# Attention and two mixer layers on one core: seven block products in place of eight in the last pair's channel products

## The chip, the cores and the metric

One NeuronCore of a Trainium2 chip runs the whole program in one launch. The metric is the device time in microseconds (us). The engines are named as in the profile: PE (matmul), PEld (PE's weight loads), DVE, ACT, POOL, and SP, which here only issues DMAs.

## The reference

Shapes: batch 4, 12 heads of 64, sequence 448, model width 768, all float32.

```python
scores = cap * tanh((q @ k.T / sqrt(64)) / cap)           # per batch and head
x = softmax(scores) @ v                                   # (4, 448, 768) after joining the heads
theta = x @ w_theta                                       # first mixer layer
y = w_tok_r @ (x * cos(theta)) + w_tok_i @ (x * sin(theta))   # over the tokens
u = x + y
x = u + relu(u @ w_ch)                                    # "wc" in the kernel
h = relu(x.T @ w_tok1) @ w_tok2                           # second layer, over the tokens
u = x + h.T
out = u + relu(u @ w_ch1) @ w_ch2                         # "c1" and "c2"; 768 -> 1536 -> 768
```

## The kernel before

Activations are held with channels on the 128 partitions and the 448 tokens along the row: `XT` holds, for two batches, six chunks of 128 channels. `XHL` holds the same values as two parts, a rounded high part and the rest. Weights are split likewise, and every product of 128x128 weights with a 128x448 chunk is three matmuls (high by high, high by low, low by high; `mm3`). An output chunk of a 768-wide product is six such steps, 18 matmuls in one PSUM bank (`gemm`).

The program goes through attention for all four batches, the mixer layers for batches 0 and 1 (the first pair, woven into the attention of batches 2 and 3), and then the same for batches 2 and 3 (the last pair), which runs alone. `token` is theta and the token mixing of the first layer; `rest` is wc, the second layer's token steps (`tok1`, `tok2`) and three channel groups (`NG`). A group is the c1 product for four output chunks and two batches (8 `gemm`s, 144 matmuls, order `CORD`) and then c2 (6 chunks, two batches, 12 matmuls each). In wc, `wch` makes one output chunk of one batch; `SEQR` is the order in which wc, `tok1` (T), `tok2` (n) and the splits (s) follow each other.

In the first pair each weight is read as raw 8-byte words, converted on ACT, DVE and POOL in pieces of 384 columns, split into high and low and stored to DRAM (`convert`); the last pair reads the split weights back, 768 KB for a unit of 128 output columns, by SP (`unit`, `weight`).

The order of instructions on every engine is made by a list scheduler in the kernel itself (`Plan`): it takes operations as they become ready, by priority, follows limited buffers (`SB` gives the count of each kind: `t` are the exponentials of the attention, 128x896, three to a pair of heads; `w` the weight units; `cw` the conversion pieces; `zx` transposed tokens), and repeats this for 30 rounds, moving work that came late forward. It covers the whole program at once, so a new buffer count or new operations anywhere may change the order elsewhere. `t` buffers are allocated in order; `av` then reads each (value product), POOL or DVE adds it into the first tile of the pair, and `sm` sums the rows.

Of the kernel before, what the change touches and what calls it, by code (L numbers as in the profile page):

```python
# [21 lines left out]
DM = H * D  # L22
P = 128
# [27 lines left out]
CORD = ((0, 0), (1, 0), (0, 1), (2, 0), (1, 1), (3, 0), (2, 1), (3, 1))  # L51
CLOSE = 1
DIR = 12
FRESH = 1
RAWS = 2
CVP = 0
ACCM = 2
# [359 lines left out]
def attn_mix_kernel(ctx: ExitStack, tc: tile.TileContext, kqd, vd, cap, wu, wtok, wt1, wt2, out):  # L417
# [244 lines left out]
    stream = order[:6] + order + order  # L662
    units = {}

    def unit(i):
        for j in range(i, min(i + (FRESH if 6 + DIR <= i < 42 else AHEAD) + 1, len(stream))):
            if j not in units:
                if 6 + DIR <= j < 42:
                    weight("u", stream[j], None, DM // CW)
                    units[j] = open_[stream[j]]  # L670
                    continue
                t = sbuf("w", "w", [2, DM], F32R)
                with pri(-100):
                    weight("u", stream[j], t, DM // CW)
                units[j] = t
        return units[i]

    XT = const("XT", [2, NC6, S])
# [165 lines left out]
        hi(h, src)  # L844
        (lo_pool if XSP[phase[0]] == "p" else lo)(l, src, h)

    def mm3(ps, wfn, xfn, n):
        for k in range(n):
            wh, wl = wfn(k)
            xh, xl = xfn(k)  # L850
            with plan.fuse():
                mm(ps, wh, xh, k == 0, False)
                mm(ps, wh, xl, False, False)
                mm(ps, wl, xh, False, k == n - 1)

    def gemm(ui, i, ps):
        w = unit(ui)
        mm3(ps, lambda k: (w[:, 0, k * P:(k + 1) * P], w[:, 1, k * P:(k + 1) * P]),
            lambda k: (XHL[:, i, k, 0, :], XHL[:, i, k, 1, :]), NC6)

    def token(pr, which):
# [59 lines left out]
            dve.tensor_tensor(out=x, in0=ps, in1=x, op=ALU.add)  # L921

        def usplit(m):
            ws = slice(which[0], which[-1] + 1)
            split(XHL[:, ws, m], XT[:, ws, m, :])

        for op in SEQ[pr].split():
            k, m = op[0], op[1:]
            if k == "w":
                if not WT or pr:  # L930
                    run(tokmix_gen(pr))
            elif k == "u":
                for j in m:
                    usplit(int(j))
            elif k == "t":
                yield from theta(int(m))
            elif k == "z":
                for i in which:
                    zt(int(m), i)
                    yield 0.75  # L940
            else:
                for i in which:
                    mix(int(m), i)
                    yield 4.3

# [8 lines left out]
    def rest(pr):  # L954
        u0 = 12 + pr * len(order)
        load_tok(pr)

        def wch(m, i):
            ps = psum("wc")[:, :S]
            gemm(u0 + m, i, ps)  # L960
            x = XT[:, i, m, :]
            dve.scalar_tensor_tensor(out=x, in0=ps, scalar=0.0, in1=x, op0=ALU.max, op1=ALU.add)
            yield 3.4

        h1s = {}

        def tok1(t, i):
            W1 = WS[1]
            xn = [sbuf("xn", "zx", [1024], F32R)[:CP] for h in range(2)]
            xn = [x.rearrange("p (c j d) -> p c j d", c=NK, j=2) for x in xn]  # L970
            for j in range(2):
                tp = psum("xp")[:CP]
                with plan.fuse():
                    for c in range(NK):
                        pe.transpose(tp[:, c * P:(c + 1) * P], XT[:, i, 2 * t + j, c * CP:(c + 1) * CP], ident)
# [9 lines left out]
            h1 = sbuf("h1", "zx", [2, 512], F32R)  # L985
            act.activation(h1[:, 0, :], ps, AF.Relu)
            dve.scalar_tensor_tensor(out=h1[:, 1, :], in0=ps, scalar=0.0, in1=f(h1[:, 0, :]), op0=ALU.max, op1=ALU.subtract)
            h1s[t, i] = h1
            yield 2.6

        def tok2(t, i):
            h1, W2 = h1s[t, i], WS[2]
            for j in range(2):
                ps = psum("t2")[:, :S]

                def hf(k):
                    s = slice(k * DT + j * P, k * DT + (j + 1) * P)
# [3 lines left out]
                x = XT[:, i, 2 * t + j, :]  # L1001
                dve.tensor_tensor(out=x, in0=ps, in1=x, op=ALU.add)
                yield 1.2

        def usplit(t, i):
            split(XHL[:, i, 2 * t:2 * t + 2], XT[:, i, 2 * t:2 * t + 2, :])

        for op in SEQR.split():
            k, m, i = op[0], int(op[1]), int(op[2])
            if k == "s":  # L1010
                usplit(m, i)
            else:
                yield from {"w": wch, "T": tok1, "n": tok2}[k](m, i)

        for g in range(NG):
            gs = {}
            v0 = u0 + 6 + 2 * FB * g
            for k, i in CORD:
                if k not in gs:
                    gs[k] = sbuf("g", "wg", [2, 2 * S], F32R).rearrange("p a (b s) -> p a b s", s=S)  # L1020
                gt = gs[k]
                ps = psum("c1")[:, :S]
                gemm(v0 + k, i, ps)
                act.activation(gt[:, 0, i], ps, AF.Relu)
                dve.scalar_tensor_tensor(out=gt[:, 1, i], in0=ps, scalar=0.0, in1=f(gt[:, 0, i]), op0=ALU.max, op1=ALU.subtract)
                yield 3.4
            for d in range(NC6):
                def wf(k):
                    n = d * FB + k
                    w = unit(v0 + FB + n // 6)  # L1030
                    s = slice((n % 6) * P, (n % 6 + 1) * P)
                    return w[:, 0, s], w[:, 1, s]

                for i in range(2):
                    ps = psum("c2")[:, :S]
                    mm3(ps, wf, lambda k: (gs[k][:, 0, i, :], gs[k][:, 1, i, :]), FB)
                    x = XT[:, i, d, :]
                    dve.tensor_tensor(out=x, in0=ps, in1=x, op=ALU.add)
                    if g == NG - 1:
                        sp_.dma_start(out[2 * pr + i, d * P:(d + 1) * P, :], x)  # L1040
                    yield 2.3

    def chain(*gens):
        for g in gens:
# [83 lines left out]
```

## Time and profile before

Three runs: median 968.26 us, 967.14 to 968.39.

| What | Value |
|---|---|
| Profiled execution, its own time | 964.5 us |
| Its span, first to last instruction | 962.7 us |
| PE busy | 949.1 us (99%), 4938 matmuls |
| PEld | 731.2 us (76%) |
| DVE, ACT, POOL busy | 532.3 (55%), 444.4 (46%), 188.4 us (20%) |
| DMA | 151.53 MB, mean 157 GB/s |
| PE idle in waits, all its rows summed | 9.7 us |
| PE's last matmul starts | 958.7 us into the span |

How to read it: the page's first part gives shares over the whole span, and the stages differ, so the windows view is read beside it, one line for each stage. PE's matmuls overlap in the records (one lasts some 366 ns, yet 144 of them take about 30 us), so the pace is taken from the length of a run of matmuls and their count.

### The profile page before, as it was taken

The page shows a single profiled execution, that of the slowest core. Times are in us where ns is not written, and L with a number is a line of the kernel's source. Part 1 is how long each engine was busy: PE and PEld are TensorE (multiplying, and loading weights), DVE is VectorE, ACT ScalarE, POOL GpSimd, SP SyncE. Part 2 cuts the span into 40 slices and gives each one's busy share as a digit, 9 for nine tenths or more (in the row PEclk, how much of TensorE's full clock was granted, in tenths as well). Part 3 has the DMA queues.
Part 4 walks back from the last instruction along what each step waited for, and adds up shares of the span by engine and source line. Part 5 has one row for each costly group of instructions (what it writes and reads, how often), then busy time and mean ns, then how long its engine had stood idle before and what let it go on. Part 6 is the DMA issues. An engine that isn't in the chain of part 4 may idle for free.

```text
span 962.7 us, 13126 instructions
## 1 busy us (share of the span) xinstructions
PE 949.1 (99%) x4938; PEld 731.2 (76%) x4938; DVE 532.3 (55%) x920; ACT 444.4 (46%) x702; POOL 188.4 (20%) x166
## 2 busy tenths in 40 slices
PE   9999999998999999999999999999999999999998
PEld 2223566554766776789999999899999889999997
DVE  7997788776776457747666592332623541212122
ACT  7787888788875446525444450332401221010010
POOL 3545233221221111002322250332200000000000
PEclk9999999999999999999999999999999999999999
DMA  7686846565537643247757589411321103323233
GB/s 252 206 273 203 258 141 193 166 209 168 189 107 214 239 117 117 73 120 247 238 184 238 185 269 322 155 66 34 110 72 60 66 1 131 103 95 131 97 121 128
DMA packets 71128, 151.53 MB, mean 157 GB/s; under 512 B 9368, under 2 KB 50456, under 8 KB 71064
## 3 DMA queue, kind: packets, MB, share of 16 engines
q1 hardware_dynamic: 71064, 150.69, 48.9%
q8 instruction: 39, 0.64, 0.3%
q14 instruction: 25, 0.20, 0.1%
HBM read 108.86 MB, written 41.68 MB: 156 GB/s over the span
## 4 chain that ended last, share of the span: by engine, by line
PE 91%; DVE 5%; DMA 2%; ACT 2%; issue 1%; POOL 0%; SPq 0%; DVEq 0%; ACTq 0%
PE c L401 36%; PE tm L401 10%; PE wc L401 9%; PE th L401 9%; PE av L401 7%; PE t L401 6%; PE sp L401 6%; PE sm L401 2%; PE tp L401 2%; DMA dn<-sr 2%; PE xp L401 2%; DVE cw L401 1%; ACT t L401 1%; DVE raw L401 1%; DVE w L401 1%
## 5 line engine op out<-in xcount | busy, mean ns | idle before, releaser
L401 PE MATMUL c<-g,w 128*128 128x448 f32 x864 | 177.2, 366 | 0.0
L401 PE MATMUL c<-XHL,w 128*128 128x448 f32 x846 | 175.6, 368 | 0.0
L401 PEld LDWEIGHTS c<-g,w 128*128 128x128 f32 x864 | 162.3, 188 | 13.9
L401 PEld LDWEIGHTS c<-XHL,w 128*128 128x128 f32 x846 | 158.7, 188 | 16.1 <-issue 0.7
L401 POOL TENSOR_TENSOR cw<-cw,raw 128x384 uint32<-128x384 uint32 (+2 forms) x94 | 92.3, 982 | 330.5 <-DVE cw L401 166.3
L401 PE MATMUL tm<-WT,zn 128*128 128x448 f32 x483 | 107.6, 372 | 2.3 <-ACT zn L401 1.8
L401 ACT ACTIVATE g<-c 128x448 fp32r<-128x448 f32 x47 | 25.7, 546 | 173.9 <-PE c L401 173.9
L401 PEld LDWEIGHTS tm<-WT,zn 128*128 128x128 f32 x483 | 88.3, 188 | 17.6 <-issue 3.5
L401 PE MATMUL th<-XHL,w 128*128 128x448 f32 x432 | 96.4, 372 | 0.0
L401 DVE TENSOR_TENSOR XT<-c,XT 128x448 f32<-128x448 f32 x72 | 44.8, 623 | 87.4 <-PE c L401 87.4
L401 PEld LDWEIGHTS th<-XHL,w 128*128 128x128 f32 x432 | 79.5, 188 | 14.9 <-issue 5.7
L401 PE MATMUL wc<-XHL,w 128*128 128x448 f32 x414 | 88.1, 368 | 0.0
L401 PEld LDWEIGHTS wc<-XHL,w 128*128 128x128 f32 x414 | 76.9, 188 | 9.6 <-issue 2.5
L401 DVE SCALAR_TENSOR_TENSOR g<-c,g 128x448 fp32r<-128x448 f32 x47 | 29.3, 622 | 99.3 <-ACT g L401 99.2
L401 ACT ACTIVATE t<-sp,consts 128x896 f32<-128x896 f32 x72 | 72.2, 1004 | 21.9 <-PE sp L401 20.5
L401 ACT ACTIVATE t<-t,consts 128x896 f32<-128x896 f32 x72 | 75.1, 1042 | 1.7
L401 PE MATMUL av<-t,vt 128*64 128x448 f32 x288 | 66.3, 558 | 0.0
L401 DVE SCALAR_TENSOR_TENSOR cw<-raw,cw 128x384 uint32<-128x384 uint32 (+2 forms) x94 | 64.3, 685 | 2.7
L401 PE MATMUL sp<-kq 64*128 64x448 f32 (+1 forms) x240 | 59.2, 574 | 2.6 <-DVE xr L401 1.9
L401 ACT CAST w<-cw 128x384 fp32r<-128x384 f32 x72 | 35.1, 508 | 45.2 <-POOL cw L401 16.5
L401 DVE TENSOR_TENSOR w<-cw,w 128x384 fp32r<-128x384 f32 x72 | 48.8, 693 | 7.2 <-ACT w L401 7.1
L401 PEld LDWEIGHTS av<-t,vt 128*64 128x64 f32 x288 | 15.8, 135 | 38.9 <-issue 35.7
(132 smaller groups left out, 1138.7 us busy)
## 6 DMA issues: line engine op xcount, KB each, us to landing
w<-cu SPq DMA_DIRECT2D x54, 768.0 KB
raw<-wu SPq DMA_DIRECT2D x72, 384.0 KB
cu<-w SPq DMA_DIRECT2D x72, 384.0 KB
kq<-kqd SPq DMA_DIRECT2D x24, 448.0 KB
vt<-vd SPq DMA_DIRECT2D x24, 224.0 KB
out<-XT SPq DMA_DIRECT2D x24, 224.0 KB
dn<-sr SPq DMA_DIRECT2D x18, 224.0 KB
raw<-wtok SPq DMA_DIRECT2D x14, 224.0 KB
```

Source lines behind the costliest of these rows:

```text
L401: getattr(eng[o.eng], name)(*map(real, a), **{x: real(y) for x, y in k.items()})
```

## The change

In the last pair, wc and c1 take their output chunks two at a time, (j, j+3) in wc and (k, k+2) in c1, for both batches together: a 2x2 block of outputs whose sum over the six input chunks is cut into two halves of three. A is the weight block (input half, output chunk), B the activation block (input half, batch). Instead of 8 block products of 9 matmuls there are 7 (`fast`), in Winograd's form of Strassen's algorithm:

- S1 = A21+A22, S3 = A11-A21, S2 = S1-A11, S4 = A12-S2 from the weights (`combine`: four reads of stored unsplit weights, 128x384 each, four POOL adds, then a high part on ACT and a low part on POOL or DVE for each), anew for every block.
- T3 = B22-B12, T2 = T3+B11, T4 = B21-T2, T1 = B12-B11 from `XT` (`sums`, `first`), split into high and low; made once for wc and once for c1, and kept in buffers that the attention has left, T1 over a part of `XHL` that the block before has finished with.
- The products, in order: A11 B11, A12 B21, S2 T2, S1 T1, S3 T3, S4 B22, A22 T4. Each is 9 matmuls in its own PSUM bank. One ACT copy and seven DVE adds combine them; then the four results go on as before.

The first block of wc and the first block of group 0 of c1 stay as four plain `gemm`s (72 matmuls), batch 1 first. So two blocks of wc and five of c1 are made by `fast`. c2 is unchanged (`mixed_group`; `FASTC2` is 0 and what it switches isn't run).

With it go: `convert` also stores the unsplit piece of 14 of the units 6 to 23; the token steps take chunks (t, t+3) together in the last pair (`both`), splits there are made for each chunk and batch alone; z and mixing take batch 1 first (`ZO`); `SEQR` has its own order for the last pair, in which W10 runs all of block 1 and W21 one product of block 2; `h1` moves from the `zx` buffers to `wg`. Buffer counts: `t` 4 to 3, `w` 3 to 4, `cw` 2 to 3, `zx` 4 to 5; `FRESH`, how many converted units are asked for ahead, 1 to 2.

```diff
-SB = {'kq': 2, 'vt': 2, 'hl': 1, 't': 4, 'tm': 2, 'sv': 2, 'dn': 1, 'xr': 2, 'pk': 3, 'rq': 2, 'w': 3, 'raw': 3, 'cw': 2, 'wg': 4, 'zx': 4, 'rc': 4}
+SB = {'kq': 2, 'vt': 2, 'hl': 1, 't': 3, 'tm': 2, 'sv': 2, 'dn': 1, 'xr': 2, 'pk': 3, 'rq': 2, 'w': 4, 'raw': 3, 'cw': 3, 'wg': 4, 'zx': 5, 'rc': 4}
-SEQR = "w00 w01 w10 w11 w20 w21 T00 w30 w31 T01 n00 w40 w41 T10 n01 w50 w51 s00 s01 T11 n10 T20 n11 s10 s11 T21 n20 n21 s20 s21"
+SEQR = ('w00 w01 w10 w11 w20 w21 T00 w30 w31 T01 n00 w40 w41 T10 n01 w50 w51 s00 s01 T11 n10 T20 n11 s10 s11 T21 n20 n21 s20 s21', 'W00 W10 T00 W21 T01 W21 n00 W21 n01 W21 T10 W22 T11 W20 s01 s00 n10 T20 n11 s11 s10 T21 n20 n21 s21 s20' if FASTWC else 'w00 w01 w10 w11 w20 w21 T00 w30 w31 T01 n00 w40 w41 T10 n01 w50 w51 s00 s01 T11 n10 T20 n11 s10 s11 T21 n20 n21 s20 s21')
+SWC = ("+ raw raw raw".split(), "+ 2 2".split())
...
+SC1 = ("+ raw raw raw".split(), "+ rc rc zx".split()) if FASTC2 else ("zx rc zx rc".split(), "zx rc zx rc".split())
+ZO = (1, 0)
+TE = "vvvp"
+TL = "vvvv"
...
+FE = "pppp"
+SL = "ppvv"
...
-FRESH = 1
+FRESH = 2
...
 def convert(key, raw, rows, n):
...
     wv = f(wv)
+        if key[0] == "u" and key[1] in plain:
+            if key[1] not in whole:
+                whole[key[1]] = dram(f"f{key[1]}", P, [DM])
+            sp_.dma_start(whole[key[1]][:, key[2] * n:(key[2] + 1) * n], wv)
...
+    def quad(a, c, fast):
+        return [("u" if not fast else "c", a, full(a)), ("u" if not fast else "c", c, half(c) if fast else full(c))]
+        stream += quad(6, 9, 0) + quad(7, 10, 1) + quad(8, 11, 1)
+    for g in range(NG):
+        n = 12 + g * FB
+        stream += quad(n, n + 2, g > 0) + quad(n + 1, n + 3, 1)
+            stream += [("u", i, full(i)) for i in order[12 + 2 * FB * g + FB:12 + 2 * FB * (g + 1)]]
+    plain = set(range(6 if FASTWC else 12, 36 if FASTC2 else 24)) - {6, 9, 12, 14}
...
+    def sums():
...
+        for k in range(H3):
+            b11, b12, b21, b22 = (XT[:, i, o + k, :] for o, i in ((0, 0), (0, 1), (H3, 0), (H3, 1)))
...
+            for e, o, x, y, op in ((TE[0], t[3], b22, b12, ALU.subtract), (TE[1], t[2], t[3], b11, ALU.add), (TE[2], t[4], b21, t[2], ALU.subtract)):
+                (pool if e == "p" else dve).tensor_tensor(out=o, in0=x, in1=y, op=op)
+            for j in (2, 3, 4):
+                h, l = pairs[f"t{j}"][k]
+                hi(h, t[j])
+                (lo_pool if TL[j - 1] == "p" else lo)(l, t[j], h)
...
+    def combine(t, srcs, N):
+        x = {}
+        with pri(-100):
+            for j, src in zip((2, 0, 1, 3), srcs):
+                x[j] = sbuf("F", "cw", [CW])[:, :N]
+                sp_.dma_start(x[j], src)
...
+        add(FE[0], s1, s3, s1)
+        add(FE[1], s3, s2, s3, ALU.subtract)
+        add(FE[2], s2, s1, s2, ALU.subtract)
+        add(FE[3], s4, s4, s2, ALU.subtract)
+        for j in (1, 2, 0, 3):
+            h, l = t[j]
+            hi(h, x[j])
+            (lo_pool if SL[j] == "p" else lo)(l, x[j], h)
...
+    def fast(A, T, post):
+        def prod(ps, a, b, first=True, last=True):
+            mm3(ps, lambda k: tuple(x[:, k * P:(k + 1) * P] for x in A[a]), lambda k: T[b][k], H3, first, last)
...
+        act.copy(p1, one("11", "b11"))
+        post(0, 0, plus(p1, one("12", "b21")))
+        dve.tensor_tensor(out=u2, in0=one("s2", "t2"), in1=p1, op=ALU.add)
+        p5 = one("s1", "t1")
+        u4 = plus(u2, p5)
+        ps = one("s3", "t3")
+        dve.tensor_tensor(out=u2, in0=ps, in1=u2, op=ALU.add)
+        post(1, 1, plus(u2, p5))
+        post(0, 1, plus(u4, one("s4", "b22")))
+        post(1, 0, plus(u2, one("22", "t4")))
...
+        def wchs(j):
...
+                for n in range(4):
+                    ps = psum("wc")[:, :S]
+                    if n == 0:
+                        T[0] = sums()
+                    gemm(u0 + n % 2, 1 - n // 2, ps)
...
+                    if n == 1:
+                        first(T[0])
+                        A4[1] = weights4(u0 + 2, SWC[0])
...
+            for n, c in enumerate(fast(A4[j], T[0], post)):
+                if n == 2 and j + 1 < H3:
+                    A4[j + 1] = weights4(u0 + 2 * j + 2, SWC[j])
...
+        def both(t):
+            return (t, t + H3) if pr and FASTWC else (2 * t, 2 * t + 1)
```

## Rows read from the trace of the kernel before

**Rows 1.** busy time of each engine by stage (windows view), columns named first

```profile
core 0: us, PE busy (x) PEld busy (x) DVE busy (x) ACT busy (x) POOL busy (x), PEclk, DMA share, GB/s
0.00:94.00 94.00, 91.14 (x455) 24.99 (x455) 81.78 (x161) 73.60 (x94) 44.13 (x39) 1.00 0.73 236
94.00:411.00 317.00, 312.18 (x1707) 208.93 (x1708) 222.99 (x390) 229.34 (x338) 66.47 (x57) 1.00 0.54 168
411.00:591.00 180.00, 180.00 (x882) 162.76 (x881) 113.74 (x196) 75.77 (x156) 49.97 (x46) 1.00 0.70 218
591.00:698.00 107.00, 106.42 (x556) 96.68 (x555) 41.93 (x65) 35.95 (x66) 27.86 (x24) 1.00 0.34 117
698.00:782.00 84.00, 82.29 (x481) 75.63 (x480) 32.60 (x48) 15.68 (x24) 0.00 (x0) 1.00 0.17 57
782.00:963.00 181.00, 177.11 (x866) 162.21 (x864) 39.21 (x63) 14.05 (x25) 0.00 (x0) 1.00 0.32 107
```

**Rows 2.** PE's waits: tile, releaser, us in total, times, longest

```profile
PE sp L401 <- DVE xr L401: 1.9, 1, 1.9
PE tm L401 <- ACT zn L401: 1.8, 2, 1.2
PE t L401 <- DVE h L401: 1.5, 2, 1.0
...
PE sp L401 <- ACT tm L401: 1.0, 1, 1.0
...
PE tm L401 <- DVE zn L401: 0.5, 1, 0.5
```

**Rows 3.** timeline of PE, end of the first pair: start, us, what, count

```profile
532.22 29.91 PE L401 MATMUL c<-XHL,w 128*128 128x448 f32 x144
561.97 29.53 PE L401 MATMUL c<-g,w 128*128 128x448 f32 x144
```

**Rows 4.** instruction groups by shape: busy us, mean ns, idle before

```profile
L401 POOL TENSOR_TENSOR cw<-cw,raw 128x384 uint32<-128x384 uint32 x72 | 75.6, 1050 | 263.2 <-DVE cw L401 138.4 <-issue 45.9 <-ACT raw L401 27.4
...
L401 DVE TENSOR_TENSOR w<-cw,w 128x384 fp32r<-128x384 f32 x72 | 48.8, 693 | 7.2 <-ACT w L401 7.1
L401 DVE TENSOR_TENSOR XT<-c,XT 128x448 f32<-128x448 f32 x72 | 44.8, 623 | 87.4 <-PE c L401 87.4
...
L401 ACT CAST w<-cw 128x384 fp32r<-128x384 f32 x72 | 35.1, 508 | 45.2 <-POOL cw L401 16.5 <-issue 12.5 <-PE c L401 8.1
...
L401 DVE TENSOR_TENSOR XHL<-XT,XHL 128x896 fp32r<-128x896 f32 x18 | 20.5, 1142 | 10.0 <-ACT XHL L401 10.0
...
L401 POOL TENSOR_TENSOR XHL<-XT,XHL 128x448 fp32r<-128x448 f32 x12 | 14.8, 1234 | 18.5 <-DVE XHL L401 18.5
...
L401 DVE TENSOR_TENSOR XHL<-XT,XHL 128x448 fp32r<-128x448 f32 x12 | 9.2, 784 | 1.6 <-ACT XHL L401 1.6
```

**Rows 5.** timeline of DVE, end of the last pair's token mixing

```profile
680.82 3.06 DVE L401 TENSOR_TENSOR XHL<-XT,XHL 128x896 fp32r<-128x896 f32 x2
683.80 0.62 DVE L401 TENSOR_TENSOR XT<-tm,XT 128x448 f32<-128x448 f32 x1
...
690.14 1.09 DVE L401 TENSOR_TENSOR XHL<-XT,XHL 128x896 fp32r<-128x896 f32 x1 [0.29 <-ACT XHL L401]
```

**Rows 6.** timeline of POOL, the same stretch

```profile
681.69 5.42 POOL L401 TENSOR_TENSOR rc<-rc,XT 128x448 f32<-128x448 f32 x4 [13.71 <-issue]
```

**Rows 7.** timeline of all engines, attention of one pair of heads

```profile
52.92 2.16 POOL L401 TENSOR_TENSOR t<-t,t 128x896 f32<-128x896 f32 x1
...
55.75 0.99 ACT L401 ACTIVATE t<-sp,consts 128x896 f32<-128x896 f32 x1
...
56.81 1.28 PE L401 MATMUL sm<-t,ones 128*32 128x448 f32 x6
...
59.16 1.00 ACT L401 ACTIVATE t<-sp,consts 128x896 f32<-128x896 f32 x1
...
63.77 0.97 PE L401 MATMUL av<-t,vt 128*64 128x448 f32 x4
```

**Rows 8.** DMA issues: destination, source, count, size

```profile
w<-cu SPq DMA_DIRECT2D x54, 768.0 KB
```

More of the change, by code (lines that the diff above doesn't have):

```diff
@@ L666, in unit @@
         for j in range(i, min(i + (FRESH if 6 + DIR <= i < 42 else AHEAD) + 1, len(stream))):
[L667 to L675, printed above, removed]
+            if j not in units and (j == i or stream[j][0] == "u"):
+                stream[j][2](j)
         return units[i]
@@ L845, in split, with mm3 @@
         (lo_pool if XSP[phase[0]] == "p" else lo)(l, src, h)
-    def mm3(ps, wfn, xfn, n):
+    def mm3(ps, wfn, xfn, n, first=True, last=True):
         for k in range(n):
@@ L851, in mm3, with first @@
             with plan.fuse():
-                mm(ps, wh, xh, k == 0, False)
+                mm(ps, wh, xh, first and k == 0, False)
                 mm(ps, wh, xl, False, False)
-                mm(ps, wl, xh, False, k == n - 1)
+                mm(ps, wl, xh, False, last and k == n - 1)
+    H3 = NC6 // 2
+    def first(pairs):
+        for k in range(H3):
+            t1 = sbuf("tf", TT[0], [S])
+            (pool if TE[3] == "p" else dve).tensor_tensor(out=t1, in0=XT[:, 1, k, :], in1=XT[:, 0, k, :], op=ALU.subtract)
+            h, l = pairs["t1"][k]
+            hi(h, t1)
+            (lo_pool if TL[0] == "p" else lo)(l, t1, h)
@@ new lines, in combine @@
+    def combine(t, srcs, N):
+        x = {}
+        with pri(-100):
+            for j, src in zip((2, 0, 1, 3), srcs):
+                x[j] = sbuf("F", "cw", [CW])[:, :N]
+                sp_.dma_start(x[j], src)
+        s1, s2, s3, s4 = (x[j] for j in range(4))
+        add = lambda e, o, x, y, op=ALU.add: (pool if e == "p" else dve).tensor_tensor(out=o, in0=x, in1=y, op=op)
+        add(FE[0], s1, s3, s1)
[6 more added lines that the diff above has]
+            (lo_pool if SL[j] == "p" else lo)(l, x[j], h)
@@ new lines, in fast2, with into @@
+    def fast2(A, T, e, close):
+        X = lambda h, i: XT[:, i, e + H3 * h, :]
+        def prod(ps, a, b, first=True, last=True):
+            mm3(ps, lambda k: tuple(x[:, k * P:(k + 1) * P] for x in A[a]), lambda k: T[b][k], 2, first, last)
+        def into(x, y, e="v"):
+            (pool if e == "p" else dve).tensor_tensor(out=x, in0=y, in1=x, op=ALU.add)
+        pa = psum("P")[:, :S]
+        prod(pa, "11", "b11", True, True)
+        p1 = sbuf("p1", "sv", [S])
+        act.copy(p1, pa)
+        for n, x in enumerate((X(1, 1), X(1, 0), X(0, 1))):
+            into(x, p1, XP[n])
+        yield 1.2
+        pd = psum("P")[:, :S]
+        prod(pd, "s4", "b22")
+        into(X(0, 1), pd)
+        yield 1.2
+        pb = psum("P")[:, :S]
+        prod(pb, "s2", "t2", True, True)
+        into(X(0, 1), pb)
+        yield 1.2
+        pc = psum("P")[:, :S]
+        prod(pc, "s1", "t1")
+        into(X(0, 1), pc)
+        close(0, 1, X(0, 1))
+        into(X(1, 1), pc)
+        yield 1.2
+        prod(pb, "s3", "t3", False, True)
+        into(X(1, 1), pb)
+        close(1, 1, X(1, 1))
+        yield 1.2
+        prod(pa, "12", "b21", False, True)
+        into(X(0, 0), pa)
+        close(0, 0, X(0, 0))
+        yield 1.2
+        prod(pb, "22", "t4", False, True)
+        into(X(1, 0), pb)
+        close(1, 0, X(1, 0))
+        yield 1.2
@@ L856, in gemm @@
+    un = [0]
     def gemm(ui, i, ps):
         w = unit(ui)
-        mm3(ps, lambda k: (w[:, 0, k * P:(k + 1) * P], w[:, 1, k * P:(k + 1) * P]),
+        mm3(ps, lambda k: (w[0][:, k * P:(k + 1) * P], w[1][:, k * P:(k + 1) * P]),
             lambda k: (XHL[:, i, k, 0, :], XHL[:, i, k, 1, :]), NC6)
@@ L923, in usplit @@
         def usplit(m):
+            if pr:
+                for i in ZO:
+                    split(XHL[:, i, m], XT[:, i, m, :])
+                return
             ws = slice(which[0], which[-1] + 1)
@@ L937, in token @@
             elif k == "z":
-                for i in which:
+                for i in (ZO if pr else which):
                     zt(int(m), i)
@@ L941, in token @@
             else:
-                for i in which:
+                for i in (ZO if pr else which):
                     mix(int(m), i)
@@ L974, in tok1 @@
                     for c in range(NK):
-                        pe.transpose(tp[:, c * P:(c + 1) * P], XT[:, i, 2 * t + j, c * CP:(c + 1) * CP], ident)
+                        pe.transpose(tp[:, c * P:(c + 1) * P], XT[:, i, both(t)[j], c * CP:(c + 1) * CP], ident)
                 tv = tp.rearrange("p (c d) -> p c d", d=P)
@@ L1000, in tok2 @@
                 mm3(ps, hf, lambda k: (W2[0][:, k, :], W2[1][:, k, :]), 2)
-                x = XT[:, i, 2 * t + j, :]
+                x = XT[:, i, both(t)[j], :]
                 dve.tensor_tensor(out=x, in0=ps, in1=x, op=ALU.add)
@@ L1005, in usplit @@
         def usplit(t, i):
+            if pr:
+                for d in both(t):
+                    split(XHL[:, i, d], XT[:, i, d, :])
+                return
             split(XHL[:, i, 2 * t:2 * t + 2], XT[:, i, 2 * t:2 * t + 2, :])
-        for op in SEQR.split():
+        gens = {}
+        for op in SEQR[pr].split():
             k, m, i = op[0], int(op[1]), int(op[2])
@@ L1011, in rest, with close, plain_group @@
                 usplit(m, i)
+            elif k == "W":
+                if m not in gens:
+                    gens[m] = wchs(m)
+                for _ in range(i or 99):
+                    c = next(gens[m], None)
+                    if c is None:
+                        break
+                    yield c
             else:
                 yield from {"w": wch, "T": tok1, "n": tok2}[k](m, i)
-        for g in range(NG):
+        def close(h, i, x, g, d):
+            if g == NG - 1:
+                sp_.dma_start(out[2 * pr + i, d * P:(d + 1) * P, :], x)
+        def plain_group(g):
             gs = {}
@@ L1043, in chain @@
+        for g in range(NG):
+            yield from (plain_group if not pr else fast_group if FASTC2 else mixed_group)(g)
     def chain(*gens):
```

245 lines of the change are left out of this document (240 added, 5 removed).

## The prediction

> **What bounds the kernel now.** I read the windows view first, cut where one stage gives way to the next: attention alone to 94 us, attention woven with the first pair to 411, that pair's channel groups to 591, then the last pair alone: token mixing to 698, wc and the token steps to 782, channel groups to the end [rows 1]. PE is busy for 91 of 94, 312 of 317, 180 of 180, 106 of 107, 82 of 84 and 177 of 181 us, always at a granted clock of 1.00, the upper of its two levels. So PE sets the time everywhere; work taken off PE is worth its own length while what feeds PE keeps up. The waits view of PE alone comes second: past the first 50 us it has five items of note, 1.9, 1.8, 1.5, 1.0 and 0.5 us [rows 2]. So there is little idle time to win, 6.7 us. In the last pair from 698 us on, where new work is put, DVE is busy for 33 of 84 and 39 of 181 us, ACT for 16 and 14, POOL for none, and the DMA share is 0.17 and 0.32 [rows 1].
>
> **The change, part by part.**
>
> *Matmuls removed.* A block of two output chunks and two batches takes 4 x 18 = 72 matmuls as it stands and 7 x 9 = 63 by the seven products. Two blocks of wc and five of c1 change: 7 x 9 = 63 matmuls fewer. Their pace, from the same kind of product: 144 matmuls from 532.22 to 561.97 us, 29.75 us, 206.6 ns each [rows 3]. 63 x 0.2066 = **13.0 us** off PE. A PSUM group shrinks from 18 matmuls to 9. That costs PE nothing that the rows show: the groups of 12 in c2 run 144 in 29.53 us including the overlap at their end, no slower than the groups of 18 [rows 3].
>
> *Work beside each new block.* A block lasts 63 x 0.2066 = 13.0 us on PE. DVE: seven adds and four results' own operations at 0.623, two low parts of 384 columns at 0.693: 11 x 0.623 + 2 x 0.693 = 8.2 us. POOL: four adds and two low parts of 384 columns at 1.05: 6.3 us. ACT: four high parts at 0.508, a copy and, in c1, four relus: under 5 us [rows 4]. All are below 13.0, so I cost them at nothing; PE covers them. If that cover went, the block would last as long as its DVE work.
>
> *DVE beside POOL.* POOL has been idle here until now, and the two disturb each other: the token mixing's two 896-column low parts took 3.06 us together while POOL multiplied, one alone took 1.09 later, so each lost about 0.44 us [rows 5, 6]. In the same stretch an add with one input from PSUM took its usual 0.62 [rows 5]. In a block six of the 13 DVE operations have both inputs in SBUF: 6 x 0.44 = 2.6 us, 10.8 us in all, still under 13.0. The Trainium skill, SBUF — State Buffer, section Who interferes with whom, states it harder: a DVE instruction with two SBUF inputs contends with a GpSimd instruction that reads SBUF, and the loser fully blocks. By that rule the full 6.3 us of POOL could come on top of DVE's 8.2; the pair of low parts above bears its direction out, not its full price. The case is a rival below.
>
> *T, made twice.* Before the first new block of wc, and again of c1, DVE makes nine sums at 0.62 and twelve low parts at 0.784, and in the same time four results (2.5) and two low parts for the weights (1.4): 5.6 + 9.4 + 2.5 + 1.4 = 18.9 us [rows 4]. What hides it is the plain block, 72 x 0.2066 = 14.9 us, and the two products that use no T, 3.7 us: 18.6 us; T1 has one more, 1.9 us. That is level, but two thirds of T use chunks that are final earlier, when DVE has room (42 of 107 us busy, 33 of 84) [rows 1]. From below it costs nothing; from above, if nothing is made early and POOL's three subtractions at 1.23 and six weight operations at 1.05 (10 us) each block DVE, some 10 us a time [rows 4]. I take 0.5 us a time, near the lower end since DVE is under half busy before both places: **+1.0 us**. Part of it stands for the token steps, whose last results now come by two DVE operations instead of one and whose splits are twelve at 0.784 in place of six at 1.142 (+2.6 us of DVE) [rows 4], beside a PE that waited there for 1.5 us already [rows 2].
>
> *Weights.* A new block reads 768 + 384 KB of split weights and 4 x 192 KB unsplit, 1.97 MB in 13.0 us, 151 GB/s, where two units of 768 KB [rows 8] served 14.9 us (106 GB/s). The last stage moves 107 GB/s now, the first pair's groups 218 beside 180 of 180 us of PE [rows 1]: cost nothing. The unsplit reads, four POOL adds and the parts take about 2 x 1.05 + 0.5 + 1.05 us after landing, and are asked for some five products (9 us) before their use. If a block ran at 107 GB/s it would last 18.4 us.
>
> *Stores in the first pair.* 28 transfers of 192 KB, 5.5 MB over the conversion of 14 units, on SP's queue and behind POOL's result; loads behind them wait with them. The third `cw` buffer covers the longer hold. There PE is never idle, at a DMA share of 0.70 [rows 1]. Cost nothing; from above the 2 us of the largest PE wait there is [rows 2].
>
> *`t` from four buffers to three.* This touches the attention, off the change's own place. In the pair of heads at 55 us a tanh starts at 55.75 into the fourth buffer. With three it would wait until the row sums of the pair before end, 56.81 + 1.28 = 58.09, so 2.3 us late; the tanh at 59.16 is then about 1 us late behind it. The value product of the first reads it at 63.77; tanh and the exp behind it take about 1.0 us each, so it would be done near 60.2, 3.6 us early [rows 7]. So the delay is absorbed and does not pass on. Nine and a half pairs run as densely as this (the first 38 steps, `FIRST`, have nothing woven in). From above, a loss of the 2.3 us in nine pairs would be 20.7 us; from below nothing. I take **+0.5 us**.
>
> *The rest.* `w`, `cw`, `zx` and `FRESH` deeper, other orders, `h1` elsewhere: same instructions. The scheduler orders the whole program anew, so the waits of rows 2 are drawn anew: between -6.7 us (all gone) and about as much more; I take 0, the middle.
>
> **Sum.** 964.5 (the profiled execution's own time) - 13.0 + 1.0 + 0.5 = 953.0. The median of the runs is 968.26, 3.76 above that execution, and the new runs should stand to theirs alike: **956.8 us**.
>
> **Rivals.**
>
> *The new draw wins too.* The deeper buffers end most of the waits of rows 2: up to 6.7 us more, 948 to 953 us. For it: they are waits on DVE and ACT results just ahead of PE, which more buffers let start sooner. Against: two of the five concern the attention, which loses a buffer.
>
> *The seams eat part.* T, splits and token steps crowd DVE around 698 and 782 us, 3 to 5 us at each place: 961 to 966. For it: 18.9 us of DVE work against 18.6 of cover. At the full 10 us a time it is 964.5 - 13.0 + 20 + 0.5 + 3.76 = 976, and slower; it decides above 13 us in all.
>
> *Slower by the attention.* Place: the dense pairs of heads before 94 us. A tanh that waits for the row sums takes its place in ACT's order, ACT is busy for 74 of 94 us and DVE for 82 [rows 1], and if nothing can be put between, PE waits 2.3 us a pair: 953.0 - 0.5 + 20.7 + 3.76 = 977. It decides when PE loses over 13 us, 1.4 us a pair. Against: the 3.6 us that remain at 63.77.
>
> *Weights late.* The saved matmuls turn into waits of PE for S parts: 5.4 us for each of c1's five blocks, 27 us: 983. Against: 218 GB/s in rows 1.
>
> *DVE held by POOL: no gain.* Each of POOL's six operations in a block holds DVE for its whole length: 8.2 + 6.3 = 14.5 us, DVE becomes the bound, and the seven blocks give back 7 x 1.5 = 10.5 of the 13.0 us: 967.3, level with before. The rule of the Trainium skill cited above would have it so. Against: 0.44 us lost per operation in rows 5, and seven of the 13 operations read PSUM.
>
> **How the numbers follow.** Forecast, 953 to 961: 0.60. New draw, 948 to 953: 0.13. Seams in part, 961 to 966: 0.10. DVE held by POOL, level: 0.04. Attention: 0.07. Seams in full: 0.03. Weights: 0.03. A measurement tells a change from none at about 0.2%, 1.9 us. Faster: 0.60 + 0.13 + 0.10 = 0.83; within: 0.04; slower: 0.13. The range 950.5 to 966 holds the forecast, the seams in part and half of the new draw, 0.77, and the ends left out are the slower cases and the best draws.
>
> **What would show it.** PE's matmuls fall from 4938 to 4875 and its busy time by 13 us, nearly all after 698 us. The groups of the first pair run as before. In a new block, runs of 9 matmuls follow without waits, and DVE is busy for 8 to 11 of 13 us, POOL for 6. PE's waits stay near 10 us in sum; new ones name `T` or `S`, low parts, or `zn`, `h` near 698 and 782 us if the seams eat it, `t` or `sp` before 94 us if the attention does, DMA into `cw` if the weights do. The prediction is wrong if the runs come within 2 us of 968, or if the 63 matmuls are gone and PE's idle time has grown by over 5 us.

## The result, and the profile after

The changed kernel's median is **956.69 us** (955.93 to 957.76, four runs) against 968.33 (967.14 to 968.46) for the kernel before on the same chip: a ratio of 0.9883, 95% interval 0.9866 to 0.9900. A second set on another chip gave 955.77 against 964.49, 0.9907 (0.9890 to 0.9924). So it is faster by 0.9 to 1.2%, and the median lies 0.1 us from the forecast. That closeness is partly luck: two of the sum's terms were wrong by almost the same amount in opposite directions, as the stages show.

The profiled execution took 957.76 us, its span is 956.0 us. First the windows view of the kernel after, cut where its own stages give way; the columns are those of [rows 1], its answer in the kernel before.

```profile
core 0: us, PE busy (x) PEld busy (x) DVE busy (x) ACT busy (x) POOL busy (x), PEclk, DMA share, GB/s
0.00:94.00 94.00, 89.48 (x446) 24.54 (x446) 81.76 (x155) 71.30 (x90) 43.05 (x38) 1.00 0.74 239
94.00:411.00 317.00, 311.74 (x1677) 203.87 (x1678) 220.35 (x397) 227.88 (x344) 71.90 (x62) 0.99 0.59 182
411.00:596.80 185.80, 185.80 (x923) 169.29 (x922) 117.19 (x196) 73.67 (x153) 52.34 (x48) 1.00 0.72 226
596.80:706.90 110.10, 107.54 (x557) 98.17 (x556) 53.47 (x83) 42.56 (x82) 33.30 (x29) 0.98 0.34 115
706.90:785.30 78.40, 78.40 (x466) 73.42 (x465) 55.18 (x89) 23.96 (x45) 12.84 (x11) 1.00 0.22 71
785.30:956.00 170.70, 166.78 (x813) 152.29 (x811) 79.76 (x120) 29.33 (x56) 31.44 (x27) 0.99 0.35 115
```

The last pair's theta begins at 596.8 us where it began at 591.3; its mixing lasts 110.1 us where it lasted 106.8; wc and the token steps last 78.4 us (84.2 before), the groups 166.8 us to PE's end (176.8). So from wc on the change gains 15.8 us, more than the 13.0 forecast, and ahead of it 8.8 us are lost. (0.6 us of both figures is only a matter of where the stages are cut: three matmuls of wc now run inside the mixing.) The granted clock is 0.99 in the woven stage (94 to 411 us) and 0.98 in the mixing, where [rows 1] shows 1.00; the 0.99 of the last stage comes from its end, behind PE's last matmul. DVE carries 79.76 us in the last stage (39.21 before), and PE has no idle time there until its last matmul.

The PE timeline of the second block of c1's middle group (start, length, what, how many matmuls) shows the seven products; the first row is A11 B11 and A12 B21 together, the last two lines are A22 T4 and the start of c2.

```profile
854.14 3.88 PE L419 MATMUL P<-XHL,w 128*128 128x448 f32 x18
857.86 2.02 PE L419 MATMUL P<-T,S 128*128 128x448 f32 x9
859.72 2.02 PE L419 MATMUL P<-XHL,S 128*128 128x448 f32 x9
861.58 2.02 PE L419 MATMUL P<-T,S 128*128 128x448 f32 x9
863.44 2.02 PE L419 MATMUL P<-XHL,S 128*128 128x448 f32 x9
865.30 2.02 PE L419 MATMUL P<-T,w 128*128 128x448 f32 x9
867.16 1.99 PE L419 MATMUL P<-g,w 128*128 128x448 f32 x9
```

A product follows every 1.86 us with no wait noted, and the block takes 867.16 - 854.14 = 13.02 us, as priced. The windows view of this block and the one before it:

```profile
841.13:854.14 13.01, 13.01 (x65) 11.83 (x64) 6.50 (x11) 4.18 (x8) 2.03 (x2) 1.00 0.41 122
854.14:867.16 13.02, 13.02 (x65) 11.83 (x64) 9.19 (x14) 3.68 (x7) 5.38 (x5) 1.00 0.46 151
```

DVE is busy for 6.5 and 9.2 of 13.0 us, POOL for 2.0 and 5.4, and the DMA moves 122 and 151 GB/s: everything beside the block fits under it.

The 8.8 us went into PE's waits and into a lower clock behind them. Ahead of theta PE is idle for 9.8 us where it was 7.7, by the windows; 1.7 of the 2.1 us more lie before 94 us (89.48 us busy against 91.14 in [rows 1]). Most of the rest of the 5.5 us is matmuls at the lower clock. PE's largest wait ends at 231.66 us. The timeline of all engines in the kernel after, with what released each idle stretch in brackets:

```profile
230.44 0.62 DVE L419 TENSOR_TENSOR xr<-xr,dn 128x448 f32<-128x448 f32 x1 [4.89 <-DMA dn<-sr]
230.99 0.62 DVE L419 COPY xr<-av 128x448 f32<-128x448 f32 x1
...
231.66 1.76 PE L419 MATMUL sp<-kq 64*64 64x448 f32 x4 [3.49 <-DVE xr L419]
...
233.35 4.52 PE L419 MATMUL th<-XHL,w 128*128 128x448 f32 x12
```

SP had issued that DMA, the softmax denominators of one pair of heads spread over the partitions, at 221.72 us:

```profile
221.72 0.52 SPq L419 DMA_DIRECT2D dn<-sr  x1
```

What it brought was used 8.7 us later. DVE works through its operations in the order that the scheduler gave it: it stood idle for 4.89 us before the one that needs this transfer; behind that one stood the copy that frees a PSUM bank (230.99 us), and PE waited 3.49 us for it. The kernel before waits in the same manner at 224 us, for 1.9 us [rows 2]. DVE's waits for this transfer (waits view: us in total, times, longest), before and after:

```profile
DVE xr L401 <- DMA dn<-sr: 34.8, 11, 4.3
```

```profile
DVE xr L419 <- DMA dn<-sr: 23.3, 10, 5.4
```

So DVE's wait is not new, and it was longer in sum before; new is that PE stood still behind one of them for 3.49 us instead of 1.94. The windows around it:

```profile
225.00:230.00 5.00, 3.17 (x20) 1.91 (x18) 0.56 (x2) 2.67 (x5) 0.00 (x0) 1.00 0.73 210
230.00:236.00 6.00, 4.34 (x11) 2.68 (x12) 5.43 (x11) 2.19 (x4) 0.00 (x0) 0.54 0.40 90
236.00:240.00 4.00, 4.00 (x19) 3.06 (x19) 0.78 (x2) 1.25 (x2) 1.01 (x1) 0.83 0.96 347
```

From about 230.5 us, still inside PE's idle stretch, to about 237.3 us the granted clock was at its lower level (0.5): 12 theta matmuls took 4.52 us where 12 x 0.2066 = 2.5 is the pace of [rows 3], so the wait cost some 2 us more there alone. In the mixing, PE's timeline shows three waits close together, and POOL's (behind it) what they waited for:

```profile
613.25 0.53 PE L419 MATMUL th<-ident,rc 128*128 128x128 f32 x3 [1.14 <-POOL rc L419]
614.33 1.09 PE L419 MATMUL tp<-ident,rc 128*128 128x128 f32 x8 [0.55 <-POOL rc L419]
616.29 9.11 PE L419 MATMUL tm<-WT,zn 128*128 128x448 f32 x36 [0.86 <-ACT zn L419]
```

```profile
609.83 8.96 POOL L419 TENSOR_TENSOR rc<-rc,XT 128x448 f32<-128x448 f32 x8 [17.81 <-ACT rc L419]
```

Here too the clock was at 0.5, from about 616.3 to 619.6 us: 36 matmuls in 9.11 us, against 7.4 at 206.6 ns.

### The profile page after: what moved, and what is told of

The parts are those of the page before. It is cut to its first block, busy times and chain, and to the rows that moved or that the text cites. A ratio compares the mean times of both kernels' runs of the same rounds, so it can differ in the third digit from the quotient of the medians.

```text
span 956.0 us, 13368 instructions
## 1 busy us (share of the span) xinstructions
PE 939.7 (98%) x4875; PEld 721.6 (75%) x4875; DVE 607.7 (64%) x1037; ACT 468.7 (49%) x769; POOL 244.9 (26%) x214
## 4 chain that ended last, share of the span: by engine, by line
PE 76%; DMA 3%; DVE 1%; ACT 0%; issue 0%; SPq 0%; DVEq 0%
PE c L419 29%; PE P L419 10%; PE tm L419 7%; PE th L419 7%; PE wc L419 7%; PE t L419 7%; PE av L419 4%; PE sp L419 3%; DMA dn<-sr 3%; PE xp L419 1%; PE tp L419 1%; DMA sr<-pk 0%; ACT rc L419 0%; DVE xr L419 0%; DVE rc L419 0%
## 5 line engine op out<-in xcount | busy, mean ns | idle before, releaser
L419 PE MATMUL c<-g,w 128*128 128x448 f32 x816 | 168.0, 366 | 0.0
L419 PEld LDWEIGHTS c<-g,w 128*128 128x128 f32 x816 | 153.3, 188 | 13.2
L419 PE MATMUL c<-XHL,w 128*128 128x448 f32 x522 | 108.1, 367 | 0.0
L419 PEld LDWEIGHTS c<-XHL,w 128*128 128x128 f32 x522 | 97.9, 188 | 9.3 <-issue 0.7
L419 DVE TENSOR_TENSOR XT<-c,XT 128x448 f32<-128x448 f32 x68 | 42.4, 623 | 82.7 <-PE c L419 82.6
L419 PEld LDWEIGHTS th<-XHL,w 128*128 128x128 f32 x432 | 81.0, 192 | 15.8 <-issue 5.1
L419 PE MATMUL wc<-XHL,w 128*128 128x448 f32 x306 | 66.4, 370 | 0.0
L419 PEld LDWEIGHTS wc<-XHL,w 128*128 128x128 f32 x306 | 56.5, 188 | 10.8 <-issue 5.3
L419 DVE SCALAR_TENSOR_TENSOR cw<-raw,cw 128x384 uint32<-128x384 uint32 (+2 forms) x94 | 61.7, 657 | 2.6
L419 DVE TENSOR_SCALAR cw<-cw 128x384 uint32<-128x384 uint32 (+2 forms) x94 | 42.0, 447 | 7.4 <-ACT cw L419 7.1
L419 PEld LDWEIGHTS sp<-kq 64*128 64x128 f32 (+1 forms) x240 | 15.9, 164 | 38.4 <-ACT t L419 13.7
```

The source lines that it names most:

```text
L419: getattr(eng[o.eng], name)(*map(real, a), **{x: real(y) for x, y in k.items()})
```

## The experiments

All runs are compared with the kernel before on their own chip (its medians: 968.33 us beside the first run of the changed kernel, 964.70, 963.36 and 964.49 us in the three later sets). Because the whole-program scheduler draws the order anew for each, the stage lengths say more than the totals. They are read off PE's timeline of one profiled execution of each kernel, in us: to the first theta matmul of the last pair, to the end of its mixing, to the end of its token steps, to PE's last matmul.

| Run | Median us | Ratio (95%) | to theta | mixing | wc, tokens | groups |
|---|---|---|---|---|---|---|
| before | | 1 | 591.3 | 106.8 | 84.2 | 176.8 |
| after | 956.69 | 0.9883 (0.9866-0.9900) | 596.8 | 110.1 | 78.4 | 166.8 |
| after_again | 955.77 | 0.9907 (0.9890-0.9924) | 594.7 | 110.2 | 78.4 | 166.8 |
| eighth_product | 967.76 | 1.0037 (1.0024-1.0050) | 595.6 | 111.6 | 82.2 | 176.3 |
| buffers_only | 970.79 | 1.0067 (1.0046-1.0089) | 595.0 | 106.8 | 84.3 | 176.8 |
| c1_only | 967.76 | 1.0032 (1.0019-1.0045) | 602.8 | 109.9 | 83.9 | 167.0 |
| wc_only | 967.47 | 1.0030 (1.0018-1.0043) | 598.3 | 109.3 | 79.3 | 175.6 |
| t_three_only | 971.89 | 1.0073 (1.0049-1.0098) | 595.9 | 106.3 | 84.2 | 176.8 |
| t_four | 956.37 | 0.9921 (0.9902-0.9939) | 596.7 | 109.4 | 78.4 | 166.8 |
| mult_order | 953.26 | 0.9884 (0.9859-0.9908) | 596.5 | 107.4 | 78.4 | 166.3 |
| sums_on_dve | 955.01 | 0.9904 (0.9884-0.9925) | 594.5 | 109.7 | 79.0 | 165.8 |
| order_dn_late | 947.75 | 0.9826 (0.9811-0.9841) | 590.6 | 106.8 | 78.5 | 165.8 |
| order_dn_xr | 956.01 | 0.9918 (0.9899-0.9938) | 595.6 | 107.4 | 78.4 | 166.7 |
| redraw | 957.75 | 0.9933 (0.9915-0.9951) | 596.8 | 109.3 | 78.4 | 166.7 |

**eighth_product.** As many matmuls as the change took away are put back, by making the first product of each block twice (it then counts double in the results); all else is kept:

```diff
-        act.copy(p1, one("11", "b11"))
+        twice = psum("P")[:, :S]
+        prod(twice, "11", "b11", True, False)
+        prod(twice, "11", "b11", False, True)
+        act.copy(p1, twice)
```

> The changed kernel with the first product of each of the seven new blocks made twice into one PSUM group, so a block has 72 matmuls again (63 more in all, 4938); its results differ, nothing else is left out. Theory, PE is the bound inside the new blocks and everything else is hidden: 63 x 0.2066 = 13.0 us more than the changed kernel, about 969.7 us, and the last pair after 698 us as long as before less the idle time it lost (the changed kernel's stage from wc to the end gained 15 us against 13.0 forecast). Rival, the blocks are set by DVE, POOL or the weights and PE has room in them: less than +6 us, under 963.

The stages grew from 78.4 to 82.2 and from 166.8 to 176.3 us: 3.8 + 9.5 = 13.3 us for 63 matmuls, 211 ns each. In PE's timeline the same block now starts with 27 matmuls and goes on at the same pace:

```profile
862.21 5.74 PE L419 MATMUL P<-XHL,w 128*128 128x448 f32 x27
867.79 2.02 PE L419 MATMUL P<-T,S 128*128 128x448 f32 x9
```

The total, 1.0037, stands 1.3 to 1.5% above the changed kernel's two ratios. PE is the bound inside the blocks; the rival (DVE, POOL or weights) falls.

**c1_only** and **wc_only.** One of the two products is left as before:

```diff
-FASTWC = 1
+FASTWC = 0
```

```diff
-        n = 12 + g * FB
-        stream += quad(n, n + 2, g > 0) + quad(n + 1, n + 3, 1)
+        stream += [("u", i, full(i)) for i in order[12 + 2 * FB * g:12 + 2 * FB * g + FB]]
...
-            yield from (plain_group if not pr else fast_group if FASTC2 else mixed_group)(g)
+            yield from (plain_group if True else fast_group if FASTC2 else mixed_group)(g)
```

> The changed kernel with wc, the order of wc and token steps and the grouping of tokens as before; the five blocks of c1 stay. Theory, each part is worth its matmuls: 45 x 0.2066 = 9.3 us off the kernel before for c1, 3.7 us lost against the changed kernel for wc's 18, so about 960.4 us, plus up to 2 us because the changed kernel also lost the 1.5 us of PE waits in the token steps. Rival, the regrouped tokens and not the 18 matmuls bring wc's share: 963 or more, with PE waits near 770 us back. Rival, wc brings nothing: 957.

> The changed kernel with c1 of the last pair as plain products in the order of the kernel before (36 matmuls of each of 12 chunks); wc's two blocks and the token grouping stay, and eight fewer units store unsplit pieces. Theory: the changed kernel plus 45 x 0.2066 = 9.3 us, about 966 us. Rival, c1's blocks are held by DVE and POOL and bring less than their matmuls: 962 or less.

Both totals missed: each part alone is slower than the kernel before by 0.3%. The stages are as the theory had them: c1 alone brings the groups to 167.0 us (9.8 of the 10.0 gained), wc alone brings its stage to 79.3 (4.9 of 5.8). In c1_only the token steps keep the waits of [rows 2], which the changed kernel lost; its waits view:

```profile
PE t L419 <- DVE h L419: 1.6, 2, 1.0
```

What spoiled both totals lies ahead of the last pair, in code that the two share with the changed kernel but for fewer stores of unsplit pieces (20 transfers in c1_only and 8 in wc_only against 28; so wc_only stores ten units fewer, not eight): theta begins at 602.8 and 598.3 us. In c1_only PE waited there 4.55 us at 249 us and 2.73 at 140, in wc_only 2.79 us at 369, and around the end of each of these waits the granted clock fell to 0.5.

**buffers_only** and **t_three_only**, on the kernel before:

```diff
-SB = {'kq': 2, 'vt': 2, 'hl': 1, 't': 4, 'tm': 2, 'sv': 2, 'dn': 1, 'xr': 2, 'pk': 3, 'rq': 2, 'w': 3, 'raw': 3, 'cw': 2, 'wg': 4, 'zx': 4, 'rc': 4}
+SB = {'kq': 2, 'vt': 2, 'hl': 1, 't': 3, 'tm': 2, 'sv': 2, 'dn': 1, 'xr': 2, 'pk': 3, 'rq': 2, 'w': 4, 'raw': 3, 'cw': 3, 'wg': 4, 'zx': 5, 'rc': 4}
...
-FRESH = 1
+FRESH = 2
```

```diff
-'t': 4
+'t': 3
```

> The kernel before with the changed buffer counts (t 3, w 4, cw 3, zx 5) and FRESH 2 alone; no block products. Theory, the gain comes from the 63 matmuls and the buffers only redraw the waits: the time of the kernel before within about 5 us, 963 to 972, PE busy as before, and the stage up to the last pair's theta not shorter than 591 us. Rival, the deeper buffers bring much of the gain: 960 or less. Rival, three t buffers stretch the attention: PE waits of over 10 us before 94 us, 975 or more.

> The kernel before with t buffers 4 to 3 and nothing else. Theory, the third t buffer is what the first part of the changed kernel lost (its last pair's theta begins at 596.8 us against 591.3, in the kernel with all changed buffer counts at 595.0): theta begins at 594 to 596 and the time is 3 to 5 us above the kernel before. Rival, the other counts (w, cw, zx, FRESH) cause it: theta at 591 to 592, time as before within 1.5 us.

The counts alone lose 3.7 us ahead of the last pair and nothing behind it; t alone loses 4.6. The totals lose more than the profiled executions do (970.79 and 971.89; the profiled ones took 968.25 and 968.59). t_three_only loses nothing in the dense attention: to 94 us PE is idle for 2.6 us there, 2.9 before. Its waits come where attention and first pair are woven, by PE's timeline:

```profile
177.38 0.97 PE L401 MATMUL av<-tm,vt 64*64 64x448 f32 x4 [1.92 <-ACT t L401]
199.72 0.57 PE L401 MATMUL av<-tm,mine 128*32 128x448 f32 x2 [1.54 <-DVE xr L401]
...
257.54 1.11 PE L401 MATMUL sp<-hl 64*128 64x448 f32 x6 [3.25 <-DVE sv L401]
```

So the rival of the prediction, attention stretched pair by pair before 94 us, is not what happens.

**t_four**, the converse on the changed kernel:

```diff
-'t': 3
+'t': 4
...
-'zx': 5
+'zx': 4
```

> The changed kernel with t back at 4 and zx at 4 (both do not fit with zx 5). Theory, the loss ahead of the last pair is the missing t buffer: theta of the last pair begins at 591 to 593 us instead of 596.8 and the time falls by 3 to 5 us. Rival, it is the new draw of the order and the wait for the denominators' DMA at 231 us, which t does not touch: theta still at 595 or later, the time unchanged within 2 us. A loss from zx would show between 596 and 707 us in the mixing, not ahead of it.

Theta still begins at 596.7: the rival held. With the fourth t back the order is another one, with waits of 2.41 us at 148 and 2.38 at 230. Taking a t away from the one order loses 4.6 us, giving it back to the other (which had to give up a `zx` buffer for it) gains nothing, so these runs show no price of the buffer itself.

**redraw.** One constant of the scheduler:

```diff
-PUSH = 15.0
+PUSH = 14.0
```

> The changed kernel with one constant of the scheduler, by how much late work is moved forward, at 14 instead of 15: the same instructions in another order. It measures what a new draw alone is worth. Theory, the stages from 707 us on keep their lengths within 0.5 us, as in all runs so far, and the start of the last pair's theta moves by up to 5 us either way from 596.8. Rival, the draws scatter about the 591 us of the kernel before too, so the changed kernel's 5.5 us there were chance: 592 or less.

The stages behind 707 us stay, theta begins at 596.8 again, by other waits. Of the twelve profiled executions of other kernels that keep the scheduler's view of that DMA, none reaches the 591.3 us of the kernel before: they lie 3.2 to 11.5 us behind it, ten of them 3.2 to 5.5. So the order before looks like a good one among those that this scheduler draws. That is argued, not shown: all twelve have some buffer count changed as well, and no run redraws the kernel before with its own counts.

**sums_on_dve.** POOL gives its share of each block to DVE:

```diff
-FE = "pppp"
-SL = "ppvv"
+FE = "vvvv"
+SL = "vvvv"
```

> The changed kernel with the four weight sums and the two low parts of each new block on DVE instead of POOL, so POOL is free from the last mixing on. By the prediction's durations DVE then has 8.2 + 6 x 0.693 = 12.4 us in a block of 13.0. Theory, PE stays the bound and POOL beside DVE cost nothing that reaches PE: the stage from 782 us to the end as in the changed kernel within 2 us, 167 us. Rival, DVE is close to its limit and its queue delays T, S or the results: 5 us or more longer, with PE waits on DVE. Rival, DVE was held by POOL: shorter by 2 us or more.

The groups last 165.8 us, 1.0 less; three of the blocks ran at 1.82 us a product instead of 1.86, which accounts for 0.8 of it. The same two blocks by the windows view:

```profile
838.52:851.29 12.77, 12.77 (x64) 11.84 (x63) 6.87 (x13) 3.71 (x7) 0.00 (x0) 1.00 0.40 125
851.29:864.06 12.77, 12.77 (x64) 11.83 (x63) 9.78 (x19) 4.29 (x8) 0.00 (x0) 1.00 0.46 154
```

DVE is far from the 12.4 us expected: 6.9 and 9.8. Its additions of 384 columns take 0.55 us there and the low parts 0.63, not the 0.69 that I took for both. POOL did hold DVE, but nothing of it reached PE. By shape, T's low parts (count, busy us, mean ns), first in the changed kernel, then without POOL's weight work:

```profile
L419 DVE TENSOR_TENSOR T<-tf,T 128x448 fp32r<-128x448 f32 x18 | 17.3, 979 | 0.6 <-ACT T L419 0.6
```

```profile
L419 DVE TENSOR_TENSOR T<-tf,T 128x448 fp32r<-128x448 f32 x18 | 12.8, 732 | 0.7 <-ACT T L419 0.6
```

The Trainium skill, SBUF — State Buffer, section Who interferes with whom, has a DVE instruction with two SBUF inputs contend with GpSimd's reads; the trace agrees in direction, 979 against 732 ns. The full blocking of every such operation that the rival priced did not come.

**mult_order.** In the last pair's theta:

```diff
-            for i in which:
+            for i in (ZO if pr else which):
                 rc = rcs[m, i]
```

> The changed kernel with one loop turned: in the last pair the products of x with cosine and sine are made for batch 1 first, in the order in which z and the mixing now take the batches. Theory: in the changed kernel z of batch 1 waits at 613 to 616 us for the third and fourth POOL product (1.19 us each) because batch 0's come first, and the granted clock then falls; with the turn the mixing stage lasts 107 us as before instead of 110, the waits on POOL rc go, and the time falls by 2 to 3.5 us. Rival, POOL is late there because the weight sums of wc queue on it: the stage stays at 109 to 110.

The mixing lasts 107.4 us. PE's timeline at the same place now has waits of 0.24 and 0.55 us, and the mixing's matmuls start at full pace:

```profile
612.57 0.55 PE L419 MATMUL tp<-ident,rc 128*128 128x128 f32 x3 [0.24 <-POOL rc L419]
613.66 0.33 PE L419 MATMUL tp<-ident,rc 128*128 128x128 f32 x1 [0.55 <-POOL rc L419]
...
614.07 2.37 PE L419 MATMUL tm<-WT,zn 128*128 128x448 f32 x9
```

So the change turned z's order to batch 1 first but left POOL making batch 0's products first. The ratio, 0.9884, does not tell it apart from the changed kernel's 0.9883 and 0.9907; the stage does.

**after_again**, **order_dn_late** and **order_dn_xr** ran with redraw as one set. The two new ones keep mult_order's loop; one tells the scheduler the truth about the DMA, the other gives it buffers:

```diff
-                            end = dma + 1.6
+                            end = dma + 1.6 + (4.0 if any(b.tag == "dn" for b in o.bufs) else 0.0)
```

```diff
-'dn': 1, 'xr': 2
+'dn': 2, 'xr': 3
...
-'zx': 5
+'zx': 4
```

> The changed kernel itself, once more, to stand on one chip beside the next three. Theory, the kernel before runs at 963 to 965 us where its wait at 224 us (1.9 us) leaves the granted clock up and at 967 to 968 where it does not, so against runs of 963 to 965 the changed kernel shows a smaller gain than the 11.6 us first measured: 6 to 9 us, about 956 to 957. Rival, the whole level differs between chips: the ratio stays 0.988.

> The changed kernel with batch 1's cosine and sine products first and, in the scheduler alone, the DMA of the softmax denominators into dn taken as landing 4 us later than it assumed (it takes 8.7 us at 222 us in the trace). Theory, the first part's loss is PE waiting at 231 us for DVE, which holds in order behind an operation on dn, and the granted clock of 0.5 after it: with the operation placed later the wait falls under 1.5 us, the clock stays up, theta of the last pair begins at 593 or earlier instead of 596.8, the mixing lasts 107 us, and the time is 5 to 7 us below the changed kernel. Rival, the order is drawn anew and other waits come in the place of this one: theta at 596 or later, only the mixing's 2.7 us gained.

> The changed kernel with batch 1's cosine and sine products first, two dn buffers, three xr buffers, and zx at 4 to make room. Theory, as DVE takes its operations in order, more buffers do not move the operation that waits for the DMA: the wait at 231 us stays at 2 us or more. Rival, the missing buffers force that order: the wait goes and theta begins at 593 or earlier.

order_dn_late is the fastest kernel here: 947.75 us, 8.0 below the changed kernel on the same chip, of which mult_order's loop accounts for about 2.7. Theta begins at 590.6, and the stretch that was at half clock is full; its windows view, and PE's largest waits:

```profile
230.00:236.00 6.00, 6.00 (x36) 4.54 (x36) 3.12 (x7) 5.87 (x8) 0.75 (x1) 1.00 0.49 134
```

```profile
PE sp L419 <- ACT t L419: 2.3, 4, 0.7
PE warm L419 <- DVE warm L419: 1.4, 1, 1.4
PE sm L419 <- DVE sv L419: 0.9, 3, 0.4
```

No single wait over 0.7 us is left behind the start. It has three `t` buffers, so the changed counts do not force the loss ahead of theta. It is a single draw: that the true DMA time, and not a lucky order, brought theta forward is likely by the other twelve, but not shown. With more buffers instead (order_dn_xr) the wait at 231 us went, against my theory, but others came in its place (2.90 us at 181, 1.82 at 250, clock down after the first), and theta begins at 595.6. after_again gained 8.7 us on its chip, as its theory had it, and its interval just excludes the rival's 0.988. It is the same program as the changed kernel, with 2.50 us at 231 where that had 3.49, half the time at the lower clock behind it, and theta 2.1 us earlier: one DMA's landing, and the clock behind it, move a run by about that much. Whether the level of the kernel before (968.33 in one set, 963.36 to 964.70 in three) comes from such a landing too was not shown. Its profiled execution at 964.5 has the clock up throughout; in the three later sets its 18 runs with a mean clock of 1.00 took 961.5 to 964.8 us and its 15 at 0.997 to 0.999 took 964.3 to 966.8, so part of its scatter goes with the clock. For the set at 968.33 the clock is not on record.

## Why the prediction was right

**Matmuls removed, -13.0.** Right: 13.3 by eighth_product. The stages from wc on gained 15.8; of the rest 1.7 us are the token steps' waits (1.5 in [rows 2]), which went with the new order of wc and tokens (1.7 us idle in c1_only's stage, none in the changed kernel's). Of the 0.8 us left, 0.6 are the three matmuls of wc that run inside the mixing, by PE's timeline of the kernel after:

```profile
699.97 0.78 PE L419 MATMUL wc<-XHL,w 128*128 128x448 f32 x3
```

PE's busy time over the whole program fell by only 9.4 us (949.1 to 939.7), not the 13 that the prediction named as a sign, since matmuls at the lower clock count longer. The time in which PE is not busy rose from 13.6 to 16.3 us, less than the 5 us that would have spoken against the prediction.

**T and the seams, +1.0.** Wrong in sign: PE waited for nothing there. T's low parts were dearer than priced (979 ns against 784), and yet PE stood still for none of them: it has no idle time from wc to its last matmul. The seams as a rival fall, and DVE held by POOL with them.

**Work beside the blocks, stores, weights, 0.** Right: 6.5 to 9.2 us of DVE in a block against 8.2 to 10.8, 122 and 151 GB/s against 151, no PE wait. In the first pair's groups, which the prediction named for the stores, PE is still never idle (185.80 of 185.80 us). (The rival of late weights adds up to 983.8, not 983.)

**t, +0.5, and the new draw, 0.** This is the step that failed. The text said that the scheduler's new draw lies between minus and plus 6.7 us, middle 0. In the orders tried it lies on one side: +3.2 to +11.5 us to theta in twelve executions, and only order_dn_late, with another DMA time in the scheduler, comes out at -0.8. Two things speak for why: the order before seems better than the scheduler's usual ones (argued only, see redraw), and the longest new waits were mostly followed by the lower clock and so paid for twice, which the sum has no term for. The changed kernel measured +5.5 where 0.5 was written. The place was wrong for the most part too: the largest piece is PE's wait at 231 us, behind DVE's in-order wait for a DMA whose data came 8.7 us after its issue, with the lower clock after it. Before 94 us PE was idle for 1.7 us more than in the kernel before, but t_three_only, which changes the `t` count alone, lost nothing there.

**Other orders, 0.** Wrong. The mixing took 3.3 us longer; 0.6 of it are wc's three matmuls, and the 2.7 us left are what mult_order got back by turning one loop. In the trace they stand as three waits (2.0 us more idle than in the kernel before) and 36 matmuls that took 1.7 us longer at the lower clock; that is 1 us more than 2.7, so the stage saved something elsewhere, and what it was stays open. I had counted its instructions and not asked whose result each z waits for.

**The offset, +3.76.** Taken from one execution of the kernel before against its median. The changed kernel's profiled execution lies 1.07 above its median. So for the profiled execution the sum gives 953.0 where 957.76 was measured, 4.8 too low, and the offset was 4.8 too high: they cancel, which is luck. By ratios the change is worth 8.7 to 11.6 us against 11.5 forecast.

## What to carry to other kernels

On an engine that is busy all the time, price removed matmuls at their traced pace; the DVE, POOL and DMA work beside them cost nothing here while it fitted in the block's length. Where one scheduler orders the whole program, a change anywhere can redraw everything: price the new draw on the losing side if the order before was a tuned one, and look at stages, not totals, since the draw can be as large as the gain. When an order of consumers is turned, turn the producers' too, and give a scheduler the DMA times that the trace shows; in the one order drawn with both, they brought 8 us, almost as much as the change.

## What the runs showed of the hardware that was not expected

A 224 KB transfer from DRAM spread over 128 partitions (dn) was used 8.7 us after its issue, with DVE idle for it, while the DMA share was 0.66.

The granted clock fell to 0.5 around the end of single PE waits of 2.38 us (t_four), 2.48 (sums_on_dve), 2.50 (after_again), 2.73 (c1_only), 2.79 (wc_only), 2.81 (mult_order), 2.90 (order_dn_xr), 3.07 (eighth_product), 3.25 (t_three_only), 3.49 (the changed kernel) and 4.55 us (c1_only). It stayed up after single waits of 2.41 (t_four too), 1.94 (before), 1.92 (t_three_only) and 1.82 us (order_dn_xr). It also fell after 1.72 and 0.54 us close together at 147 us (redraw), and after the 1.14, 0.55 and 0.86 us close together in the mixing, but stayed up after 1.47 and 1.32 us at the same place in the mixing (redraw). So the length of one wait alone does not say here whether the clock falls.

The same nine matmuls took 1.82 us in some blocks and 1.86 in others; nothing tried here tells why.
